# Linear attention with a gated MLP: a mixed second-stage list, maxima copies on VectorE, k and q by half batch

## The chip, the cores and the metric

The kernel runs on one core of a Trainium2 chip. The metric is the device time of one execution in microseconds (us); lower is better. A profiled execution gives the trace from which all rows below come. Engines are named as the profile names them: PE is TensorE's matmuls, PEld its weight loads, DVE is VectorE, ACT is ScalarE, POOL is GpSimd, SP is SyncE, which here only issues DMAs.

## What is computed

Eight batches of eight heads, 576 tokens, head size 64. First an attention with exponential features, then a gated MLP over the 512 joined columns.

```
phi(x)  = [exp(p), exp(-p)],  p = x @ w_phi - max|x @ w_phi|     # 64 -> 128 -> 256 features
kv      = phi(k)^T @ v ;  z = sum over tokens of phi(k)
x       = (phi(q) @ kv) / (phi(q) @ z + 1e-6)                    # per head
h       = relu(x @ w_in) ;  u, v = the two halves of h           # 512 -> 1024
v_n     = (v - mean) / sqrt(var + 1e-6)
out     = (u * (w_spatial @ v_n + b_spatial)) @ w_out
```

## The kernel before

Of a batch's 576 tokens, 512 are the main part, four blocks of 128, and 64 are the tail; the tails of two batches make one tile of 128. The first stage works in 36 **units**: per batch four head pairs (`pj` 0 to 3), and per pair of batches one tail unit. A loop over steps runs, at step i, the keys and queries of unit i, the maxima of unit i-1, the features and sums of unit i-2, the attention of unit i-3 and the output transpose of unit i-4 (`ORDER`, `LAGS`, lines 588 to 593). A middle step lasts some 6.7 us.

**Loads.** k and q of a batch come in bfloat16 through casting DMAs on POOL's queue, one DMA of all eight heads each (`load`, L90), into tiles with two buffers each; v comes in float32 through SP (`load_v`). They are issued 6 and 5 steps before the batch's first unit, those of a tail 5 and 4 steps before its unit (lines 650 to 676). Batches 0 and 1, the tails, are transposed on PE (`a_transpose`, L227). From batch 2 on, SP issues a DMA transpose of the whole batch's k and one of q, three steps ahead (`cross`, L105), into kT_b and qT_b, and one step before each unit a copy of half of qT into another tile (`q_even`, L223).

**Maxima.** For the units of batches 2 to 7 (`merged`), the eight heads' maxima of q, in a high and a low part, go through a PE transpose and are copied into spare partitions of two tiles that are the moving operands of the feature matmuls (L325): VectorE copies the odd one out of PSUM (L311), then POOL copies the odd one into the even one (L312).

**The second stage** of a batch is a list of tasks, made when its first stage ends (`b_tasks`, L571) and appended to one queue. After each kind of first-stage work, `fill` (L597) adds a credit in proportion to the queue's length and takes tasks from the front while the credit is at least half of the next one's cost (some 0.85 us for four matmuls of 512 columns). A task of cost 0 goes with whatever is ahead of it. The tasks are: v projections (four blocks and the tail: matmuls L428, ReLU L430, statistics L431 and L432), the normalise (a root on POOL, L438 to L441, and four multiply-adds on POOL, L445), u projections (four, L482, ReLU L484, into uT, which has one buffer), the u tail, spatial products (four, each of five matmuls, L503 and L504, which read all four normalised blocks; gate on VectorE, L506), the spatial tail, and output projections (four, L528; an odd batch adds the tail's). The copies of outputs out of PSUM alternate between VectorE and ACT (L531). Output projections of a batch are held back into the next batch's list.

**Order.** [...]DMA issues marked with `pin` keep the order of the program; other instructions are ordered ahead of time by a scheduler, mostly as the program has them. All matmul outputs share eight PSUM banks.

Of the kernel before, what the change touches and what calls it, by code (L numbers as in the profile page):

```python
# [8 lines left out]
FP32 = mybir.dt.float32  # L9
BF16 = mybir.dt.bfloat16  # L10
# [6 lines left out]
def kernel(  # L17
# [42 lines left out]
    def pin(start):  # L60
        return lambda *a, **kw: tc.keep_in_program_order(start(*a, **kw))

    def main_ap(t, b, h0=0, n=H):
        return bass.AP(tensor=t.tensor, offset=t.offset + (b * H + h0) * S * D,
                       ap=[[NB * D, P], [S * D, n], [1, NB * D]])
# [9 lines left out]

    def alloc(b):
        st[b] = dict(
            q=ld.tile([P, H, NB * D], BF16, tag="q_bf", name="q_bf", bufs=2),
            k=ld.tile([P, H, NB * D], BF16, tag="k_bf", name="k_bf", bufs=2),
            v=ld.tile([P, H * NB, D], FP32, tag="v_f", name="v_f"),  # L80
        )

# [4 lines left out]
            v=ld.tile([P, H, D], FP32, tag="v_tl", name="v_tl", bufs=1),  # L87
        )

    def load(x, b, h0=0, n=H):  # L90
        if b not in st:
            alloc(b)
        pin(nc.gpsimd.dma_start)(out=st[b][x][:, h0:h0 + n], in_=main_ap(q if x == "q" else k, b, h0, n))

    def load_v(b, eng):
        pin(eng.dma_start)(out=st[b]["v"].rearrange("p (h c) d -> p h (c d)", h=H), in_=main_ap(v, b))

    def load_tail(x, g):
        if g not in gs:
# [2 lines left out]
        for i in range(2):  # L102
            pin(eng.dma_start)(out=gs[g][x][i * TL:(i + 1) * TL], in_=tail_ap(t, 2 * g + i))

    def cross(b):  # L105
        d = st[b]
        for x in ("k", "q"):
            d[x + "T"] = ld.tile([P, 2 * H, P], BF16, tag=x + "T_b", name=x + "T_b", bufs=2)
            pin(nc.sync.dma_start_transpose)(out=d[x + "T"], in_=d[x].rearrange("p h x -> p (h x)"))


    wphi_f = cpool.tile([P, F], FP32)
# [32 lines left out]
    pin(nc.vector.tensor_scalar)(out=sel, in0=sel1.unsqueeze(2).to_broadcast([P, H, F]), scalar1=-1.0,  # L145
                                 scalar2=None, op0=ALU.mult)
    for x in ("k", "q"):
        pin(nc.vector.tensor_copy)(out=st[0][x][:, 0:2], in_=first[x])
    vst, vnt = [], []
    for i in range(2):  # L150
        t = cpool.tile([P, 2, 2, H, DA], BF16, name=f"vst{i}")
# [7 lines left out]
        for bl, row in ((0, TL), (1, 0)):  # L159
            pin(nc.scalar.copy)(out=t[:, bl, :], in_=ident[:, row:row + 1].to_broadcast([P, HALF]))  # L160
        vnt.append(t)
    load_v(0, nc.sync)
    for x in ("k", "q", "v"):
        load_tail(x, 0)
    load("k", 0, 2, 2)
    load("q", 0, 2, 2)
    load("k", 0, 4, 4)
    load("q", 0, 4, 4)

    w_in_bf = cpool.tile([P, KC, DFF], BF16)  # L170
    w_out_bf = cpool.tile([P, KC, DM], BF16)
    wsp = s2.tile([P, NB, T0], BF16, tag="vn", name="wsp", bufs=2)
    wspr = cpool.tile([P, NB, TL], BF16)
    wspt = ld.tile([TL, S], BF16, tag="kT_b", name="wspt", bufs=2)
    bsp_row = ld.tile([P, S], FP32, tag="qT_b", name="bsp_row", bufs=2)
    nc.sync.dma_start(out=bsp_row[TL:TL + 1, :], in_=moe_b_spatial)
    nc.sync.dma_start(out=bsp_row[0:1, :], in_=moe_b_spatial)

# [43 lines left out]

    def q_even(u):  # L223
        u["qE"] = qts[u["i"] % len(qts)]
        pin(nc.sync.dma_start)(out=u["qE"][0:D], in_=st[u["b"]]["qT"][0:D, 4 * u["pj"]:4 * u["pj"] + 4, :])

    def a_transpose(u):  # L227
        src = st[u["b"]] if u["pair"] else gs[u["g"]]
        if "kT" in src:
            for x in ("kT", "qT"):  # L230
                u[x] = src[x][:, 4 * u["pj"]:4 * u["pj"] + 4, :] if u["pair"] else src[x]
            return
        for x, copy in (("k", nc.vector.tensor_copy if u["i"] < EK else nc.scalar.copy), ("q", nc.vector.tensor_copy)):
            pt = psum.tile([P, 4, P], BF16, tag="bank", name="pt")
            for j in range(4):
                if u["pair"]:
                    blk = src[x][:, 2 * u["pj"] + j // 2, (j % 2) * P:(j % 2 + 1) * P]
                else:
                    blk = src[x][:, 2 * j:2 * j + 2, :]
                nc.tensor.transpose(out=pt[:, j, :], in_=blk, identity=ident)  # L240
            u[x + "T"] = a1.tile([P, 4, P], BF16, tag="kT", name="kT") if x == "k" else qts[u["i"] % len(qts)]
            copy(out=u[x + "T"], in_=pt)
# [63 lines left out]
    def a_max_t(u):  # L306
        pt = psum.tile([P, P], BF16, tag="bank", name="pt")
        nc.tensor.transpose(out=pt, in_=mhl[u["i"] % NM], identity=ident)
        if merged(u):
            odd, even = u["qT"][0:2 * H], u["qE"][D:D + 2 * H]  # L310
            nc.vector.tensor_copy(out=odd, in_=pt[0:2 * H, :].unsqueeze(1).to_broadcast([2 * H, 4, P]))  # L311
            nc.gpsimd.tensor_copy(out=even, in_=odd)  # L312
            return
        nc.vector.tensor_copy(out=mT[u["i"] % NM][0:2 * H, :], in_=pt[0:2 * H, :])

# [118 lines left out]
    def root(mv, r, n):  # L434

        var = small.tile([P, NB, 1], FP32, tag="var", name="var")
        rs = small.tile([P, NB, 2], FP32, tag="rs", name="rs")
        nc.gpsimd.tensor_scalar(out=var[r, 0:n], in0=mv[r, 0:n, 1:2], scalar1=1e-6, scalar2=None, op0=ALU.add)  # L438
        nc.gpsimd.tensor_tensor(out=rs[r, 0:n, 0:1], in0=var[r, 0:n], in1=neghalf[r, 0:n].unsqueeze(2), op=ALU.pow)
        nc.gpsimd.tensor_tensor(out=var[r, 0:n], in0=mv[r, 0:n, 0:1], in1=rs[r, 0:n, 0:1], op=ALU.mult)  # L440
        nc.gpsimd.tensor_scalar(out=rs[r, 0:n, 1:2], in0=var[r, 0:n], scalar1=-1.0, scalar2=None, op0=ALU.mult)  # L441
        return rs

    def normalize(dst, src, rs):
        nc.gpsimd.tensor_scalar(out=dst, in0=src, scalar1=rs[:, 0:1], scalar2=rs[:, 1:2],  # L445
                                op0=ALU.mult, op1=ALU.add)

    def b_v(b, j):
        d = st[b]
        if j == 0:  # L450
            d["vn"] = s2.tile([P, NB, HALF], BF16, tag="vn", name="vn", bufs=2)
            d["mv"] = small.tile([P, NB, 2], FP32, tag="mv", name="mv")
            d["vr"] = {}
        d["vr"][j] = s2.tile([P, HALF], BF16, tag="vr", name="vr", bufs=5)
        stats = small.tile([P, 6], FP32, tag="stats", name="stats")
        v_mm(lambda kc: d["xT"][:, kc, j * P:(j + 1) * P], d["vr"][j], slice(0, P), stats, d["mv"][:, j, :])

    def b_ln(b):
        d = st[b]
        rstd = root(d["mv"], slice(0, P), NB)  # L460
        for j in range(NB):
            normalize(d["vn"][:, j, :], d["vr"][j], rstd[:, j, :])

    def b_v_tail(g, bls):
        d = gs[g]
        r = slice(bls[0] * TL, (bls[-1] + 1) * TL)
        vr = s2.tile([P, HALF], BF16, tag="vr", name="vr", bufs=5)
        stats = small.tile([P, 6], FP32, tag="stats", name="stats")
        mv = small.tile([P, 1, 2], FP32, tag="mv_t", name="mv_t")
        v_mm(lambda kc: d["xTt"][:, kc, r], vr, r, stats, mv[:, 0, :])  # L470
        rstd = root(mv, r, 1)
        for bl in bls:
            r = slice(bl * TL, (bl + 1) * TL)
            normalize(vnt[g % 2][r, bl, :], vr[r], rstd[r, 0, :])
# [90 lines left out]
    def out_tasks(b):  # L565
        ts = [(MM, lambda j=j: b_o(b, j)) for j in range(NB)]
        if b % 2:
            ts.append((MM, lambda: b_o_tail(b // 2, [0, 1])))
        return ts

    def b_tasks(b):  # L571

        g, bl = b // 2, b % 2
        held = out_tasks(b - 1) if b else []
        ts = held[:2]
        ts.append((MM, lambda: b_v_tail(g, [bl])))
        ts += [(MM, lambda j=j: b_v(b, j)) for j in range(NB)]
        ts.append((0.0, lambda: b_ln(b)))
        ts += held[2:]
        if b == 0:  # L580
            ts += [(0.3, lambda i=i: transpose_spatial(i)) for i in range(NB + 1)]
        ts += [(MM, lambda dc=dc: b_u(b, dc)) for dc in range(KC)]
        ts.append((MM / 2, lambda: b_u_tail(g, [bl])))
        ts += [(MS, lambda dc=dc: b_s(b, dc)) for dc in range(KC)]
        ts.append((MS / 2, lambda: b_s_tail(g, [bl])))
        return ts + (out_tasks(b) if b == B - 1 else [])

# [65 lines left out]
    def at(i, f, *a):  # L653
        io.setdefault(i, []).append(lambda: f(*a))

    at(1, load, "k", 1)
    at(1, load, "q", 1)
    at(1, load_v, 1, nc.sync)
    at(2, load_weight, w_in_bf[:, :, HALF:DFF], cols[:, :, HALF:DFF])
    at(3, load_weight, wsp, rows[:, :, 0:T0])  # L660
    at(3, load_weight, wspr, rows[:, :, T0:S])
# [2 lines left out]
    at(4, load_weight, w_in_bf[:, :, 0:HALF], cols[:, :, 0:HALF])  # L664
    at(4, load_weight, w_out_bf, moe_w_out.rearrange("(kc p) f -> p kc f", p=P))
    for u in units:
        if not u["pair"] and u["g"] > 0:
            at(u["i"] - AT, load_tail, "k", u["g"])
            at(u["i"] - AT + 1, load_tail, "q", u["g"])
            at(u["i"] - AT + 1, load_tail, "v", u["g"])  # L670
        if u["pair"] and u["pj"] == 0 and u["b"] > 1:
            at(u["i"] - AB, load, "k", u["b"])
            at(u["i"] - AB + 1, load, "q", u["b"])
            at(u["i"] - AB + 1, load_v, u["b"], nc.sync)
            if u["b"] >= XB:
                at(u["i"] - XP, cross, u["b"])
    at(7, weights_with_max)
    for u in units:
        if merged(u):
# [37 lines left out]
```

## Time and profile before

| | us |
|---|---|
| median of 13 runs | 288.94 |
| lowest to highest | 286.95 to 298.14 |
| the profiled execution's own time | 288.7 |
| its span, first to last instruction | 286.9 |
| POOL: vs multiplies (L287), 64 of 1.04 us | 65.4 |
| POOL: even maxima copies (L312), 24 of 0.60 us | 14.5 |
| POOL: issuing k and q of the main part (L61), 18 | 16.3 |
| POOL: normalises (L445), 32 of 0.77 us | 24.2 |
| DMA: median from issue to landing, k_bf / q_bf / kT_b / qT_b / xT | 8.0 / 7.5 / 6.6 / 4.8 / 3.4 |

A row of a profile's groups has the line, the engine and the operation, the tile written and those read, the shapes and the number of instructions. A row of waits has who waited for whom, the microseconds in total, how often, and the longest. A row of the timeline has start and duration in us. A row of a stretch has, after its bounds and its length, the busy time of PE, PEld, DVE, ACT and POOL with instruction counts, the granted clock, the DMA share and GB/s.

### The profile page before, as it was taken

What the parts mean: (1) busy time and instruction counts of PE and PEld (TensorE: products, weight loads), DVE (VectorE), ACT (ScalarE), POOL (GpSimd) and SP (SyncE); (2) the same over time, 40 slices, a digit from 0 to 9 for tenths busy, and PEclk for the clock granted to TensorE, in tenths of its full rate; (3) what the DMA queues carried; (4) which work ended last, traced back from release to release, by engine and by line L of the source; (5) the groups of instructions that cost most, each with busy time, mean ns of one, the idle gap of its engine ahead of it and who ended that gap; (6) DMA issues with size and microseconds to landing.
All of it is one profiled execution on the core that took longest, in us unless ns stands there. A gap on an engine that the chain in (4) does not pass through costs nothing.

```text
span 286.9 us, 8120 instructions
## 1 busy us (share of the span) xinstructions
PE 259.0 (90%) x3042; PEld 171.7 (60%) x3042; DVE 220.6 (77%) x551; ACT 222.4 (77%) x504; POOL 203.1 (71%) x368
## 2 busy tenths in 40 slices
PE   3168899989899989999999989999999999999993
PEld 2057776766576565667666666666666775554441
DVE  6279998878698967899798968887879796655441
ACT  7649999998598996899889977899879967833601
POOL 8569998089966998789858996789568953420710
PEclk9999999999999999999999999999999999999999
DMA  7989999999555998999939998999732211212105
GB/s 182 215 161 121 208 220 222 167 196 163 71 99 156 218 210 91 152 302 165 194 84 146 257 187 148 223 160 178 161 110 66 68 20 73 75 39 74 74 2 184
DMA packets 83628, 41.90 MB, mean 146 GB/s; under 512 B 50626, under 2 KB 78978, under 8 KB 83588
## 3 DMA queue, kind: packets, MB, share of 16 engines
q1 hardware_dynamic: 56100, 29.90, 46.9%
q0 software_dynamic: 27328, 11.41, 33.3%
q8 instruction: 24, 0.39, 0.6%
q14 instruction: 16, 0.13, 0.2%
q10 hardware_dynamic: 160, 0.07, 0.1%
HBM read 32.85 MB, written 9.44 MB: 147 GB/s over the span
## 4 chain that ended last, share of the span: by engine, by line
PE 56%; POOL 14%; DVE 12%; ACT 9%; DMA 4%; issue 3%; POOLq 0%; ACTq 0%; DVEq 0%
PE ps L503 8%; PE po L528 8%; PE pv L428 7%; PE pu L482 6%; PE ps L247 5%; DMA q_tl<-in_q_dram 4%; PE pv L359 4%; ACT kf L262 4%; ACT qf L346 3%; PE pq L325 3%; PE pn L379 3%; POOL vn L445 3%; DVE mk L259 3%; DVE stats L431 2%; PE ps L504 2%
## 5 line engine op out<-in xcount | busy, mean ns | idle before, releaser
L262 ACT ACTIVATE kf<-ps 128x512 bf16<-128x512 f32 x144 | 75.5, 644 | 9.3 <-DVE mk L259 9.1
L287 POOL TENSOR_TENSOR vs<-v_f,em 128x512 bf16<-128x512 f32 x64 | 65.4, 1042 | 17.0 <-ACT em L282 11.6
L346 ACT ACTIVATE qf<-pq 128x512 bf16<-128x512 f32 x128 | 66.3, 617 | 11.2 <-PE pq L325 10.7
L259 DVE TENSOR_REDUCE mk<-ps 128x4 f32<-128x512 f32 x72 | 45.8, 672 | 0.6 <-PE ps L247 0.3
L273 DVE TENSOR_REDUCE mq<-ps 128x4 f32<-128x512 f32 x62 | 39.6, 678 | 4.9 <-PE ps L247 4.1
L503 PE MATMUL ps<-w_spT,vn 128*128 128x512 bf16 x128 | 34.3, 380 | 2.9 <-POOL vn L445 2.9
L506 DVE TENSOR_TENSOR uT<-ps,uT 128x512 bf16<-128x512 f32 x32 | 22.0, 687 | 19.2 <-PE ps L504 19.2
L431 DVE BATCH_NORM_STATS2 stats<-vr 128x6 f32<-128x512 bf16 (+1 forms) x40 | 26.7, 681 | 7.0 <-ACT vr L430 6.7
L482 PE MATMUL pu<-xT,w_in_bf 128*128 128x512 bf16 x128 | 31.4, 379 | 0.3 <-ACT kf L262 0.3
L528 PE MATMUL po<-w_out_bf,uT 128*128 128x512 bf16 x128 | 31.4, 379 | 0.0
L428 PE MATMUL pv<-w_in_bf,xT 128*128 128x512 bf16 x128 | 31.2, 379 | 0.0
L430 ACT ACTIVATE vr<-pv 128x512 bf16<-128x512 f32 (+1 forms) x40 | 23.7, 629 | 7.3 <-PE pv L428 6.6
L370 DVE TENSOR_TENSOR x<-pn,rc 128x256 bf16<-128x256 f32 x64 | 25.1, 419 | 0.5
L359 PE MATMUL pv<-vs,kf 128*128 128x66 bf16 x512 | 24.5, 193 | 0.6 <-DVE mq L273 0.4
L445 POOL TENSOR_SCALAR vn<-vr,rs 128x512 bf16<-128x512 bf16 x32 | 24.2, 766 | 0.8
L379 PEld LDWEIGHTS <-qf 128*128 128x128 bf16 x512 | 20.0, 97 | 7.9 <-ACT qf L346 1.1
L531 ACT COPY ob<-po 128x512 f32<-128x512 f32 x18 | 11.2, 621 | 16.3 <-PE po L528 10.0
L484 ACT ACTIVATE uT<-pu 128x512 bf16<-128x512 f32 x32 | 19.5, 638 | 5.3 <-PE pu L482 5.1
L359 PEld LDWEIGHTS <-kf 128*128 128x128 bf16 x512 | 21.8, 97 | 2.9 <-issue 2.0
L379 PE MATMUL pn<-kv,qf 128*128 128x66 bf16 x512 | 21.7, 193 | 0.9 <-ACT qf L346 0.9
L361 PE MATMUL pv<-vst,kf 128*128 128x66 bf16 x128 | 21.2, 192 | 1.1 <-POOL vst L304 1.1
L302 POOL TENSOR_TENSOR vst<-v_tl,em 64x512 bf16<-64x512 f32 x16 | 16.3, 1037 | 5.5 <-ACT em L282 5.3
(128 smaller groups left out, 563.0 us busy)
## 6 DMA issues: line engine op xcount, KB each, us to landing
v_f<-in_v_dram SPq DMA_DIRECT2D x8, 1024.0 KB, 10.5
out_dram<-ob SPq DMA_DIRECT2D x32, 256.0 KB, 2.6
k_bf<-in_k_dram POOLq DMA_DIRECT2D x7, 512.0 KB, 8.0
q_bf<-in_q_dram POOLq DMA_DIRECT2D x7, 512.0 KB, 7.5
qt<-qT_b SPq DMA_DIRECT2D x24, 64.0 KB, 3.7
v_tl<-in_v_dram SPq DMA_DIRECT2D x8, 128.0 KB, 7.5
w_in_bf<-in_moe_w_in_dram POOLq DMA_DIRECT2D x2, 512.0 KB, 8.3
out_dram<-ob SPq DMA_DIRECT2D x8, 128.0 KB, 2.4
```

The costliest lines, as they stand in the source:

```text
L259: nc.vector.tensor_reduce(out=u["mk"][:, hs], in_=pk, axis=AX.X, op=ALU.max, apply_absolute_value=True)
L262: nc.scalar.activation(out=u["kf"][:, s, hs, :], in_=pk, func=AF.Exp, bias=0.0, scale=sc)
L273: nc.vector.tensor_reduce(out=mq[:, 4 * half:4 * half + 4], in_=pq, axis=AX.X, op=ALU.max, apply_absolute_value=True)
L287: nc.gpsimd.tensor_tensor(out=vs[:, s, :, 0:D], in0=st[u["b"]]["v"][:, pj * H:(pj + 1) * H, :], in1=em[:, s, :].unsqueeze(2).to_broadcast( ...
L346: nc.scalar.activation(out=qf[:, s], in_=pq, func=AF.Exp, bias=0.0, scale=sc)
L359: nc.tensor.matmul(out=pv[:, hh, s, :], lhsT=u["kf"][:, s, 4 * hh + c, :], rhs=u["vs"][:, s, 4 * hh + c, :], start=(c == 0), stop=False)
L379: nc.tensor.matmul(out=pn[:, pos, :], lhsT=u["qf"][hh][:, s, pos, :], rhs=d["kv"][:, 2 * u["pj"] + hh, s, :], start=(s == 0), stop=(s == 1))
L428: nc.tensor.matmul(out=pv[r], lhsT=lhs(kc), rhs=w_in_bf[:, kc, HALF:DFF], start=(kc == 0), stop=(kc == KC - 1))
L445: nc.gpsimd.tensor_scalar(out=dst, in0=src, scalar1=rs[:, 0:1], scalar2=rs[:, 1:2], op0=ALU.mult, op1=ALU.add)
L482: nc.tensor.matmul(out=pu, lhsT=w_in_bf[:, kc, dc * P:(dc + 1) * P], rhs=d["xT"][:, kc, :], start=(kc == 0), stop=(kc == KC - 1))
L503: nc.tensor.matmul(out=ps, lhsT=d["vn"][:, sp, cs], rhs=w_spT[:, sp, 0:T0], start=(sp == 0), stop=False)
L528: nc.tensor.matmul(out=po[r], lhsT=lhs(dc), rhs=w_out_bf[:, dc, :], start=(dc == 0), stop=(dc == KC - 1))
```

## The change

Four things. (1) The list of a batch is ordered anew: the held outputs stand one by one ahead of the v tail, between the second and third v projection, and in turns with normalises and u projections; the root and the four normalises are tasks of their own. (2) The even copy of the maxima is made by VectorE. (3) k and q of batches 1 to 7 are loaded as two DMAs of four heads, into four half-size tiles per tensor with a buffer each, used in turns, one DMA a step; v of batches 2 to 7 comes as two DMAs, into the same tile. The tail loads of batches 4 and 6 (with 5 and 7) start one step earlier. (4) The DMA transposes are made per unit, three steps before it, 48 of a quarter of the size. Two small weight tiles that shared buffers with kT_b and qT_b share them with other tiles.

```diff
-        st[b] = dict(q=ld.tile([P, H, NB * D], BF16, tag="q_bf", bufs=2), k=..., v=...)
+        st[b] = dict(q=[None, None], k=[None, None], v=...)
...
+    def half_tile(x, b, y):
...
+            n = f"{x}_bf{(2 * b + y) % 4}"
+            st[b][x][y] = ld.tile([P, 4, NB * D], BF16, tag=n, name=n, bufs=1)
...
-    def cross(b):
-        d = st[b]
-        for x in ("k", "q"):
-            d[x + "T"] = ld.tile([P, 2 * H, P], BF16, tag=x + "T_b", name=x + "T_b", bufs=2)
-            pin(nc.sync.dma_start_transpose)(out=d[x + "T"], in_=d[x].rearrange("p h x -> p (h x)"))
+    def cross(x, u):
+        n = f"{x}T_b{u['b'] % 2}{u['pj']}"
+        u[x + "T"] = ld.tile([P, 4, P], BF16, tag=n, name=n, bufs=1)
+        src = st[u["b"]][x][u["pj"] // 2][:, 2 * (u["pj"] % 2):2 * (u["pj"] % 2) + 2, :]
+        pin(nc.sync.dma_start_transpose)(out=u[x + "T"], in_=src.rearrange("p h x -> p (h x)"))
...
-            nc.gpsimd.tensor_copy(out=even, in_=odd)
+            nc.vector.tensor_copy(out=even, in_=odd)
...
-        held = out_tasks(b - 1) if b else []
-        ts = held[:2]
-        ts.append((MM, lambda: b_v_tail(g, [bl])))
-        ts += [(MM, lambda j=j: b_v(b, j)) for j in range(NB)]
-        ts.append((0.0, lambda: b_ln(b)))
-        ts += held[2:]
+        outs = out_tasks(b - 1) if b else []
+        vs = [(MM, lambda j=j: b_v(b, j)) for j in range(NB)]
+        us = [(MM, lambda dc=dc: b_u(b, dc)) for dc in range(KC)]
+        ss = [(MS, lambda dc=dc: b_s(b, dc)) for dc in range(KC)]
+        ns = [(0.0, lambda j=j: b_ln(b, j)) for j in range(NB)]
+        ts = outs[:1] + [(MM, lambda: b_v_tail(g, [bl]))] + vs[:2] + outs[1:2] + vs[2:]
+        ts.append((0.0, lambda: b_root(b)))
         if b == 0:
             ts += [(0.3, lambda i=i: transpose_spatial(i)) for i in range(NB + 1)]
-        ts += [(MM, lambda dc=dc: b_u(b, dc)) for dc in range(KC)]
-        ts.append((MM / 2, lambda: b_u_tail(g, [bl])))
-        ts += [(MS, lambda dc=dc: b_s(b, dc)) for dc in range(KC)]
+        for y in range(NB):
+            ts += ns[y:y + 1] + outs[2 + y:3 + y] + us[y:y + 1]
+        ts += [(MM / 2, lambda: b_u_tail(g, [bl]))] + ss
...
-    at(1, load, "k", 1)
-    at(1, load, "q", 1)
+    at(1, load, "k", 1, 0)
+    at(1, load, "q", 1, 0)
+    at(1, load, "k", 1, 1)
+    at(1, load, "q", 1, 1)
...
+            early = 1 if u["g"] > 1 else 0
+            at(i - AT - early, load_tail, "k", u["g"])
+            for x in ("q", "v"):
+                at(i - AT + 1 - early, load_tail, x, u["g"])
+        if u["pair"] and u["b"] >= XB:
+            if u["pj"] == 0:
+                for n, (x, y) in enumerate((("k", 0), ("q", 0), ("k", 1), ("q", 1))):
+                    at(i - AB + n, load, x, u["b"], y)
+                for y in range(2):
+                    at(i - AB + 1 + 2 * y, load_v, u["b"], y)
+            for x in ("k", "q"):
+                at(i - XP, cross, x, u)
```

More of the change, by code (lines that the diff above doesn't have):

```diff
@@ L77, in alloc @@
         st[b] = dict(
-            q=ld.tile([P, H, NB * D], BF16, tag="q_bf", name="q_bf", bufs=2),
-            k=ld.tile([P, H, NB * D], BF16, tag="k_bf", name="k_bf", bufs=2),
+            q=[None, None], k=[None, None],
             v=ld.tile([P, H * NB, D], FP32, tag="v_f", name="v_f"),
@@ L88, in alloc_tail, with load, load_v @@
         )
-    def load(x, b, h0=0, n=H):
+    def half_tile(x, b, y):
         if b not in st:
             alloc(b)
-        pin(nc.gpsimd.dma_start)(out=st[b][x][:, h0:h0 + n], in_=main_ap(q if x == "q" else k, b, h0, n))
-    def load_v(b, eng):
-        pin(eng.dma_start)(out=st[b]["v"].rearrange("p (h c) d -> p h (c d)", h=H), in_=main_ap(v, b))
+        if st[b][x][y] is None:
+            n = f"{x}_bf{(2 * b + y) % 4}"
+            st[b][x][y] = ld.tile([P, 4, NB * D], BF16, tag=n, name=n, bufs=1)
+        return st[b][x][y]
+    def load(x, b, y, h0=0, n=4):
+        t = half_tile(x, b, y)
+        pin(nc.gpsimd.dma_start)(out=t[:, h0:h0 + n], in_=main_ap(q if x == "q" else k, b, 4 * y + h0, n))
+    def load_v(b, y=None):
+        if b not in st:
+            alloc(b)
+        h0, n = (0, H) if y is None else (4 * y, 4)
+        pin(nc.sync.dma_start)(
+            out=st[b]["v"][:, h0 * NB:(h0 + n) * NB, :].rearrange("p (h c) d -> p h (c d)", h=n),
+            in_=main_ap(v, b, h0, n))
     def load_tail(x, g):
@@ L147 @@
     for x in ("k", "q"):
-        pin(nc.vector.tensor_copy)(out=st[0][x][:, 0:2], in_=first[x])
+        pin(nc.vector.tensor_copy)(out=half_tile(x, 0, 0)[:, 0:2], in_=first[x])
     vst, vnt = [], []
@@ L161 @@
         vnt.append(t)
-    load_v(0, nc.sync)
+    load_v(0)
     for x in ("k", "q", "v"):
         load_tail(x, 0)
[L165 to L168, printed above, removed]
+    load("k", 0, 0, 2, 2)
+    load("q", 0, 0, 2, 2)
+    load("k", 0, 1)
+    load("q", 0, 1)
     w_in_bf = cpool.tile([P, KC, DFF], BF16)
@@ L173 @@
     wspr = cpool.tile([P, NB, TL], BF16)
-    wspt = ld.tile([TL, S], BF16, tag="kT_b", name="wspt", bufs=2)
-    bsp_row = ld.tile([P, S], FP32, tag="qT_b", name="bsp_row", bufs=2)
+    wspt = s2.tile([TL, S], BF16, tag="ob", name="wspt", bufs=6)
+    bsp_row = s2.tile([P, S], FP32, tag="xT", name="bsp_row", bufs=3)
     nc.sync.dma_start(out=bsp_row[TL:TL + 1, :], in_=moe_b_spatial)
@@ L224, in q_even @@
         u["qE"] = qts[u["i"] % len(qts)]
-        pin(nc.sync.dma_start)(out=u["qE"][0:D], in_=st[u["b"]]["qT"][0:D, 4 * u["pj"]:4 * u["pj"] + 4, :])
+        pin(nc.sync.dma_start)(out=u["qE"][0:D], in_=u["qT"][0:D])
     def a_transpose(u):
+        if u["pair"] and u["b"] >= XB:
+            return
         src = st[u["b"]] if u["pair"] else gs[u["g"]]
[L229 to L232, printed above, removed]
         for x, copy in (("k", nc.vector.tensor_copy if u["i"] < EK else nc.scalar.copy), ("q", nc.vector.tensor_copy)):
@@ L236, in a_transpose @@
                 if u["pair"]:
-                    blk = src[x][:, 2 * u["pj"] + j // 2, (j % 2) * P:(j % 2 + 1) * P]
+                    blk = src[x][u["pj"] // 2][:, 2 * (u["pj"] % 2) + j // 2, (j % 2) * P:(j % 2 + 1) * P]
                 else:
@@ L456, in b_v, with b_root, b_ln @@
         v_mm(lambda kc: d["xT"][:, kc, j * P:(j + 1) * P], d["vr"][j], slice(0, P), stats, d["mv"][:, j, :])
-    def b_ln(b):
+    def b_root(b):
+        st[b]["rs"] = root(st[b]["mv"], slice(0, P), NB)
+    def b_ln(b, j):
         d = st[b]
-        rstd = root(d["mv"], slice(0, P), NB)
-        for j in range(NB):
-            normalize(d["vn"][:, j, :], d["vr"][j], rstd[:, j, :])
+        normalize(d["vn"][:, j, :], d["vr"][j], d["rs"][:, j, :])
     def b_v_tail(g, bls):
@@ L654, in at @@
         io.setdefault(i, []).append(lambda: f(*a))
-    at(1, load, "k", 1)
-    at(1, load, "q", 1)
-    at(1, load_v, 1, nc.sync)
+    at(1, load, "k", 1, 0)
+    at(1, load, "q", 1, 0)
+    at(1, load, "k", 1, 1)
+    at(1, load, "q", 1, 1)
+    at(1, load_v, 1)
     at(2, load_weight, w_in_bf[:, :, HALF:DFF], cols[:, :, HALF:DFF])
@@ L666 @@
     for u in units:
+        i = u["i"]
         if not u["pair"] and u["g"] > 0:
[L668 to L676, printed above, removed]
+            early = 1 if u["g"] > 1 else 0
+            at(i - AT - early, load_tail, "k", u["g"])
+            for x in ("q", "v"):
+                at(i - AT + 1 - early, load_tail, x, u["g"])
+        if u["pair"] and u["b"] >= XB:
+            if u["pj"] == 0:
[5 more added lines that the diff above has]
+                at(i - XP, cross, x, u)
     at(7, weights_with_max)
```

## The prediction

> **What bounds the kernel now.** I read the shares of busy time first, then the busy time by stretch, then the list of waits, then the timeline around the longest of them.
>
> ```profile
> PE 259.0 (90%) x3042; PEld 171.7 (60%) x3042; DVE 220.6 (77%) x551; ACT 222.4 (77%) x504; POOL 203.1 (71%) x368
> ```
>
> TensorE (PE) is busiest, but its ends are modelled, so the stretches say more. The columns are length, then PE, PEld, DVE, ACT and POOL busy.
>
> ```profile
> 0.00:20.00 20.00, 7.78 (x46) 5.13 (x47) 10.44 (x33) 12.15 (x21) 13.14 (x30) 1.00 1.08 199
> 20.00:60.00 40.00, 35.96 (x533) 28.60 (x532) 37.38 (x106) 37.29 (x89) 31.15 (x49) 1.00 1.20 177
> 60.00:80.00 20.00, 17.25 (x201) 11.67 (x199) 14.52 (x38) 15.08 (x35) 18.75 (x35) 1.00 0.82 139
> 80.00:110.00 30.00, 27.91 (x360) 18.94 (x358) 24.98 (x61) 25.61 (x62) 24.29 (x44) 1.00 0.94 173
> 110.00:160.00 50.00, 49.71 (x606) 33.51 (x606) 43.42 (x104) 44.41 (x103) 40.94 (x76) 1.00 0.96 168
> 170.00:260.00 90.00, 89.44 (x1065) 58.12 (x1063) 71.98 (x177) 71.16 (x161) 58.75 (x109) 1.00 0.55 109
> ```
>
> From 110 us on PE is the bound: 49.7 of 50 and 89.4 of 90. It idles 12.2 us in the first 20 (the first loads), 4.0 in the opening up to 60, 2.8 in 60:80, where POOL is busy 18.75 of 20, and 2.1 in 80:110. A change that moves no matmul can win only there and in the short waits of later batches. The waits name the cause:
>
> ```profile
> POOL k_bf L61 <- DMA kT_b<-k_bf: 6.6, 1, 6.6
> PEld L503 <- POOL vn L445: 5.7, 9, 0.8
> PE ps L503 <- POOL vn L445: 2.9, 8, 0.5
> PE pq L325 <- POOL qt L312: 2.1, 2, 1.4
> ```
>
> Where TensorE waits in the middle, it waits for POOL. Two pieces of the timeline:
>
> ```profile
> 71.55 0.39 PE L503 MATMUL ps<-w_spT,vn 128*128 128x512 bf16 x1 [0.53 <-POOL vn L445]
> 72.31 0.39 PE L503 MATMUL ps<-w_spT,vn 128*128 128x512 bf16 x1 [0.36 <-POOL vn L445]
> 73.06 0.39 PE L503 MATMUL ps<-w_spT,vn 128*128 128x512 bf16 x1 [0.36 <-POOL vn L445]
> 73.81 0.39 PE L503 MATMUL ps<-w_spT,vn 128*128 128x512 bf16 x1 [0.36 <-POOL vn L445]
> ```
>
> Four matmuls start 0.76 us apart, where running ones of this size start 0.22 apart: 4 x 0.54 = 2.2 us lost for batch 0's normalised values. POOL was late because it stood 6.64 us before the k load of batch 3, issued at 57.85.
>
> ```profile
> 101.48 0.27 PE L325 MATMUL pq<-qt,wm 128*128 128x128 bf16 x2 [1.43 <-POOL qt L312]
> ```
>
> Here TensorE waits for the even copy of the maxima, which had stood on POOL behind a root.
>
> [...]at 71.55 to 73.81 the row looks half busy, yet it delivers a third of its rate. [...]a quarter-size one (xT) lands in 3.4 us, the full one (kT_b) in 6.6[...].
>
> **The change, part by part.** Sum against the profiled execution's own 288.7 us (span 286.9 and 1.8 around it), which is 0.24 below the median of 288.94.
>
> *Even copies to VectorE.* They take 24 x 0.602 = 14.5 us off POOL. The two waits of TensorE for qt, 2.1 us, go: the new copy follows the odd one on the same engine. **Gain 2.1** (bounds 1.5 to 2.1). [...]Queued behind it are the key and query maxima that ACT's Exps and the next transposes wait for. [...]At 87% (110:160) TensorE lost next to nothing; at 93% (20:60) it lost 10%, mostly for other causes. I take **1.2 us on the path**, bounds 0 and 6.
>
> *Half loads.* Batches 1 to 7: 28 issues for 14. A full issue takes POOL 0.93 (median of k_bf), the half ones at the start took 0.80: 28 x 0.80 - 14 x 0.93 = +9.4 us on POOL, so net 9.4 - 14.5 = -5.1. In the opening the four issues of batch 1 add 1.3 us to a POOL that is almost never idle from 20 to 48; TensorE there waits for ACT and VectorE more, so **cost 0.4** (0 to 1.3). The first half of batch 1's q lands earlier: TensorE waited 0.8 us for it at 31: **gain 0.6** (0 to 0.8). The k load of batch 3 no longer shares a two-buffer tag with batch 2 but has its own buffer, last read by TensorE's transposes of batch 1, done by 45.2. Then POOL's 6.64 us should go and with it the 2.2 us for batch 0's vn: **gain 2.0** (0 to 2.2). The tail loads of batches 4 and 6 move a step ahead of the k load: before, six issues, 4.8 us of POOL, stood between 150 and 161, its root came 5.4 us after its statistics, and TensorE lost 2 x 0.54 at 168 to 169: **gain 1.0** (0 to 1.1).
>
> *Transposes.* 48 of a quarter size for 12 full ones; SP's issue time goes from 43.9 us (the sum of the 12) to 48 x 1.25 (median of xT) = 60, plus 6 v halves at 0.55: +19 us of SP over 190. Moved past on SP: outputs, xT and q_even. Each pair's transposes start three steps, some 20 us, before its keys; landing 3.4 hides. Cost 0; without that cover, up to 2.
>
> *The list.* Matmuls are the same. Up to the last v, and from there to the spatial product, the same tasks stand: the last v to the spatial product is 5.6 us of second-stage matmuls in both lists. Only the normalises move: n3 was queued right after the last v, some 11.5 us ahead of the spatial product (155.47 to 167.16 in batch 3); now only u3 and the u tail lie between, 1.33/5.6 x 11.5 = 2.7 us. n3 takes 0.77, so it is in time while POOL runs less than 1.95 us late. From statistics to root POOL was late by 8.7, 1.8, 1.9, 5.4, 1.7, 0.7, 0.2 and 0.15 us; the two large ones are what the loads cure. **Cost 0.6** (0 to 9). A new wait: uT has one buffer, and the fourth held output of the previous batch, which still reads it, now comes after u0; u0's ReLU waits for that output's matmuls, 0.86 us, and what lies between. Behind it on ACT stand Exps; other PSUM banks cover it. **Cost 0.6** in seven batches (0 to 6). The drain at the end (262 to 284) has the same work after its last v: 0.
>
> **Sum.** Gains 2.1 + 0.6 + 2.0 + 1.0 = 5.7; costs 1.2 + 0.4 + 0.6 + 0.6 = 2.8; 288.7 - 2.9 = **285.8 us**.
>
> **Rivals.** *Late normalises, slower.* If POOL runs 3.2 us late at n3 (a vs pair of 2.08, a load of 0.8, a mhl pair), the spatial product waits 3.2 - 1.95 = 1.25 us in seven batches, 8.8 instead of 0.6: 285.8 + 8.2 = **294.0**. For it: n3 stood ready only 0.7 to 3.7 us ahead even when queued 9 us sooner. Against: POOL loses 5 us of work and bursts are spread. It decides from a lateness of 1.95; the sum turns slower beyond 1.95 + 3.5/7 = 2.45.
> [...]
> *POOL's wait for a transpose stays, a smaller gain.* If the 6.64 us are not due to the shared buffers, 2.0 stays: **287.8**. For it: batch 3's load has no need of batch 2's buffer as I read the code, so the wait isn't understood.
> *It doesn't do what it says*: by the diff u and spatial are not in turns; all four spatial tasks still follow the u tail. No sum above counts on turns.
>
> **Chances.** Forecast 0.48; small gain 0.12; no change 0.14; slower 0.26. A measurement of this kernel tells about 0.3% from no change, 0.87 us: faster means under 288.07. That gives faster 0.48 + 0.10 = 0.58, same 0.02 + 0.14 = 0.16, slower 0.26. The likeliest case alone spans 283.5 to 287.5. All gains at no cost give 288.7 - 5.7 = 283.0, and with the other 1.0 us of 60:80 282.0; upward the range takes in a third of the slower rival's spread (290 to 297): 282.0 to 292.0.
>
> **What would show it.** Right: no wait of TensorE for qt; [...]POOL's 6.6 us wait gone and its busy time near 198; 60:80 with under 1 us idle. Wrong: waits for vn over 9 us in sum or in every batch (late normalises); [...]ACT waiting before uT for po; PE waiting for kT or qT (SP).

## The result and the profile after

The changed kernel takes **284.84 us** (median of 11 runs, 283.0 to 286.13), the kernel before, beside it, 289.33 (48 runs): the ratio is **0.985** [0.983, 0.988]. A second measurement gave 284.0, ratio 0.980 [0.978, 0.983]. The forecast was 285.8, in a range of 282 to 292, with faster as the likeliest sign. Ratios here are taken over undisturbed runs, so that one can differ a little from the quotient of the medians shown. Brackets are 95% intervals.

The profiled execution has 284.84 us, too, and a span of 283.0, 3.9 less than before. First the shares of busy time of the changed kernel:

```profile
PE 258.7 (91%) x3042; PEld 172.4 (61%) x3042; DVE 229.6 (81%) x575; ACT 223.1 (79%) x504; POOL 198.5 (70%) x358
```

VectorE has 9.0 us more than before, POOL 4.6 less. By stretch (columns as before: length, then PE, PEld, DVE, ACT, POOL):

```profile
20.00:60.00 40.00, 36.28 (x528) 28.52 (x526) 37.37 (x103) 36.85 (x91) 38.67 (x61) 1.00 1.23 170
60.00:80.00 20.00, 18.88 (x234) 13.47 (x234) 16.74 (x46) 17.31 (x40) 15.52 (x28) 1.00 0.96 151
80.00:110.00 30.00, 28.90 (x360) 19.72 (x357) 27.30 (x67) 26.72 (x63) 25.57 (x46) 1.00 1.04 169
110.00:160.00 50.00, 50.00 (x607) 33.51 (x606) 46.43 (x113) 45.14 (x106) 39.66 (x72) 1.00 1.11 169
```

The idle time of PE in 60:80 falls from 2.75 to 1.12 us, in 80:110 from 2.09 to 1.10, in 110:160 from 0.29 to none, 2.9 us in all. These are the stretches at which the prediction aimed. In a second profile of the changed kernel (after_2) they are 1.34, 1.38 and 0.53, only 1.9 us less than before, though that execution took the same time between the points compared below. So such sums of idle time are good to about 1 us. The waits of the changed kernel (L513 and L454 are the spatial product and the normalise; before they were L503 and L445):

```profile
PEld L513 <- POOL vn L454: 1.2, 2, 0.7
...
PE ps L513 <- POOL vn L454: 0.4, 1, 0.4
```

The wait of POOL for a k load (6.6 us), the waits of TensorE for qt (2.1), and most of those for vn (5.7 and 2.9 on the two PE rows) are gone. POOL's multiplies now wait 21.3 us for ACT (11.6 before): POOL has become early instead of late.

**A second measure.** The first 20 us depend on when the first loads land, and by 18 us the profiles lie up to 2.6 us apart. So I also compare points inside the traces: the end of the first ReLU of a v projection (ACT writing vr), and, as a milestone of each batch, the end of its fourth gate multiply (VectorE writing uT from ps). The changed kernel and a_copy were profiled twice; between points these repeated to 0.1 us. The kernel before was profiled once.

| kernel | first v at | batch 0 at | batch 7 at | first v to batch 0 | batch 0 to 7 |
|---|---|---|---|---|---|
| before | 51.4 | 82.2 | 278.2 | 30.8 | 196.0 |
| fixed k and q buffers (b_tags) | 51.1 | 79.7 | 275.8 | 28.6 | 196.1 |
| all but list and copy (b_half) | 51.5 | 80.1 | 275.0 | 28.6 | 194.9 |
| all but the list (a_list) | 52.9 | 82.0 | 277.3 | 29.0 | 195.3 |
| all but the copy (a_copy, a_copy_2) | 51.6, 50.9 | 80.2, 79.5 | 272.6, 271.9 | 28.6, 28.6 | 192.4, 192.4 |
| the whole change (after, after_2) | 52.1, 51.6 | 81.1, 80.7 | 274.4, 274.0 | 29.0, 29.0 | 193.3, 193.3 |

From the first v to batch 7 the change takes off 4.5 us (226.8 to 222.3). Loads and transposes give 3.3 of them (before against b_half), the list 2.5 (b_half against a_copy), and the copy costs 1.3 (a_copy against after). With the copy made first and the list after it, the copy costs 0.8 and the list gives 2.0.

### The profile page after: what moved, and what is told of

The parts are those of the page before. It is cut to its first block, busy times and chain, and to the rows that moved or that the text cites. A ratio compares the mean times of both kernels' runs of the same rounds, so it can differ in the third digit from the quotient of the medians.

```text
span 283.0 us, 8167 instructions
## 1 busy us (share of the span) xinstructions
PE 258.7 (91%) x3042; PEld 172.4 (61%) x3042; DVE 229.6 (81%) x575; ACT 223.1 (79%) x504; POOL 198.5 (70%) x358
## 3 DMA queue, kind: packets, MB, share of 16 engines
q1 hardware_dynamic: 57348, 29.90, 51.6%
## 4 chain that ended last, share of the span: by engine, by line
PE 62%; DVE 11%; DMA 9%; ACT 8%; POOL 5%; issue 2%; POOLq 0%; ACTq 0%; DVEq 0%
PE ps L513 10%; PE pv L437 9%; PE po L538 8%; PE pu L492 7%; PE ps L256 6%; DMA q_tl<-in_q_dram 4%; PE pv L368 4%; PE pn L388 4%; ACT kf L271 3%; DMA k_bf<-in_k_dram 3%; DVE mk L268 3%; PE pq L334 3%; PE ps L514 2%; DVE stats L440 2%; DMA xT<-x 2%
## 5 line engine op out<-in xcount | busy, mean ns | idle before, releaser
L296 POOL TENSOR_TENSOR vs<-v_f,em 128x512 bf16<-128x512 f32 x64 | 65.5, 1044 | 22.7 <-ACT em L291 21.3
L268 DVE TENSOR_REDUCE mk<-ps 128x4 f32<-128x512 f32 x72 | 47.7, 677 | 2.6 <-PE ps L256 1.8
L513 PE MATMUL ps<-w_spT,vn 128*128 128x512 bf16 x128 | 33.2, 379 | 0.5 <-POOL vn L454 0.4
L538 PE MATMUL po<-w_out_bf,uT 128*128 128x512 bf16 x128 | 32.4, 379 | 0.0
L492 PE MATMUL pu<-xT,w_in_bf 128*128 128x512 bf16 x128 | 32.1, 379 | 0.0
L454 POOL TENSOR_SCALAR vn<-vr,rs 128x512 bf16<-128x512 bf16 x32 | 24.3, 766 | 1.1
```

Of the source, the lines that this page charges most:

```text
L268: nc.vector.tensor_reduce(out=u["mk"][:, hs], in_=pk, axis=AX.X, op=ALU.max, apply_absolute_value=True)
L296: nc.gpsimd.tensor_tensor(out=vs[:, s, :, 0:D], in0=st[u["b"]]["v"][:, pj * H:(pj + 1) * H, :], in1=em[:, s, :].unsqueeze(2).to_broadcast( ...
L492: nc.tensor.matmul(out=pu, lhsT=w_in_bf[:, kc, dc * P:(dc + 1) * P], rhs=d["xT"][:, kc, :], start=(kc == 0), stop=(kc == KC - 1))
L513: nc.tensor.matmul(out=ps, lhsT=d["vn"][:, sp, cs], rhs=w_spT[:, sp, 0:T0], start=(sp == 0), stop=False)
L538: nc.tensor.matmul(out=po[r], lhsT=lhs(dc), rhs=w_out_bf[:, dc, :], start=(dc == 0), stop=(dc == KC - 1))
```

## Experiments

My theory: POOL's wait for a buffer and its bursts of work made normalised values and maxima late; the loads cure that, the copy on VectorE adds to it, the list costs a little. Rivals: the list by itself makes the normalises late; the copy is what pays or what hurts; POOL's wait had nothing to do with the shared buffers.

### One part of the change at a time, on the kernel before

**b_copy**: the even copy on VectorE, alone.

```diff
-            nc.gpsimd.tensor_copy(out=even, in_=odd)
+            nc.vector.tensor_copy(out=even, in_=odd)
```

> The kernel before with the even copy of the maxima on VectorE, nothing else. Own theory (POOL was late, the copy's place cost TensorE two waits): -0.9 us, the 2.1 us of waits for qt gone, some of it taken back by VectorE; POOL's 6.6 us wait stays. [...]Rival (the new list brought the gain): no change.

Measured: median 294.1, ratio 1.010 [1.007, 1.013], **slower**. No branch of the expectation had the reason. The waits for qt did go, and VectorE's copies averaged 0.37 us. But TensorE now waits for xT, the input of the v projections. From the waits of b_copy:

```profile
PE pv L428 <- DMA xT<-x: 5.8, 2, 4.1
```

Rows of POOL and of SP's queue in b_copy (start, duration):

```profile
114.01 0.95 POOL L61 DMA_DIRECT2D k_bf<-in_k_dram  x1 [0.28 <-issue]
...
114.05 2.40 SPq L61 DMA_TRANSPOSE qT_b<-q_bf  x1
...
117.79 2.78 SPq L388 DMA_TRANSPOSE xT<-x  x2
```

The same place in the kernel before:

```profile
116.65 2.72 SPq L388 DMA_TRANSPOSE xT<-x  x2
...
116.82 0.61 POOL L312 COPY qt<-qT_b 16x512 bf16<-16x512 bf16 x1
117.38 0.95 POOL L61 DMA_DIRECT2D k_bf<-in_k_dram  x1
```

In both kernels the whole-batch transpose of q stands at the head of SP's queue and waits for the load of q, and two small transposes of xT queue behind it: SP issues nothing from 105.1 to 113.59 before, and from 106.5 to 114.05 here. So this hold is not what the copy's move changed. What changed is the load of the next k. In the kernel before it stands on POOL behind a pair of vs multiplies and an even copy, and goes out 0.7 us after the first transpose of xT. Without the copy it stands ahead of the pair, and goes out 3.8 us before that transpose. From issue to landing of the first xT there, b_copy, then before:

```profile
DMA to landing us min/median/max: 7.5/7.5/7.5
...
DMA to landing us min/median/max: 3.4/3.4/3.4
```

The transpose of q takes longer to land, too, 9.2 us instead of 4.4. TensorE comes to its v projection only 0.9 us earlier than before (120.40 against 121.28); xT lands 5.2 us later (125.26 against 120.02). Two batches on it is the same: 6.7 us with the k load first, 2.5 in the kernel before with xT first. That the k load slows the transposes is read from this order; no run moved the load alone. PE in b_copy at the first place:

```profile
125.31 0.61 PE L428 MATMUL pv<-w_in_bf,xT 128*128 128x512 bf16 x1 [4.09 <-DMA xT<-x]
...
127.52 3.49 PE L428 MATMUL pv<-w_in_bf,xT 128*128 128x512 bf16 x8
```

TensorE loses 4.09 us, and then eight matmuls take 3.49, 0.44 each instead of 0.22. In 123.90:130.70 the granted clock is 0.50: half clock for 6.8 us, from 1.4 us before the wait ends. In a_ns below, a wait of 2.12 us has half clock behind it for 3.4 us (105.90 to 109.30; mean clock 0.99 over that execution), while waits of 1.76 and 2.39 us in b_tagcopy have none (mean clock 1.0 over that execution). What brings the clock down is not shown. This execution took 295.75, so its stalls are larger than the median's; the same wait stands in b_tagcopy, in an execution at its median.

**b_list**: the new list and its split of root and normalises, alone (the part on `b_tasks` of the diff above; `b_ln` is split into `b_root` and one normalise a call).

```diff
...
-        ts.append((0.0, lambda: b_ln(b)))
-        ts += held[2:]
+        ts.append((0.0, lambda: b_root(b)))
...
+        for y in range(NB):
+            ts += ns[y:y + 1] + outs[2 + y:3 + y] + us[y:y + 1]
...
```

> The kernel before with the new list of tasks, nothing else. Own theory: the list gains nothing by itself and costs up to 1.2 us, because normalises stand later behind a POOL that is still late: 0 to +1.2 us, waits for vn at least as long as before (8.6 us of both kinds). Rival (mixing the kinds brought the gain): -2 to -4 us.

Measured: 292.81, ratio 1.011 [1.006, 1.016], **slower**, by some 3 us, where at most 1.2 was expected. This is my slower rival's mechanism. The waits of b_list:

```profile
PEld L504 <- POOL vn L445: 9.8, 11, 1.7
...
PE ps L504 <- POOL vn L445: 7.2, 8, 1.4
```

And POOL in b_list between the first and the last normalise of batch 1:

```profile
103.80 0.77 POOL L445 TENSOR_SCALAR vn<-vr,rs 128x512 bf16<-128x512 bf16 x1
...
106.90 2.08 POOL L287 TENSOR_TENSOR vs<-v_f,em 128x512 bf16<-128x512 f32 x2
...
109.11 0.78 POOL L445 TENSOR_SCALAR vn<-vr,rs 128x512 bf16<-128x512 bf16 x1
...
111.72 0.77 POOL L445 TENSOR_SCALAR vn<-vr,rs 128x512 bf16<-128x512 bf16 x1
```

In the kernel before, the four ran in one piece from 101.53 to 104.55, and this same burst (two tail loads, a q load, a vs pair) came after them. With the split list it comes between them: the last starts 7.9 us after the first.

**b_tags**: two fixed buffers each for k and q, by the batch's parity, in place of two from a shared pool; whole loads and everything else as before.

```diff
-            q=ld.tile([P, H, NB * D], BF16, tag="q_bf", name="q_bf", bufs=2),
+            q=ld.tile([P, H, NB * D], BF16, tag=f"q_bf{b % 2}", name="q_bf", bufs=1),
```

(k likewise.)

> The kernel before with k and q in two fixed buffers (one for even, one for odd batches) instead of a pool of two; same loads, same memory. Own theory (the 6.6 us wait of POOL came from which buffer the pool gave out): the wait is gone and with it the late normalises of batch 0, -2.0 us. Rival (the wait belongs to the size or the time of the loads): the wait stays, no change.

Measured: 286.1, ratio 0.989 [0.984, 0.993], **faster**. POOL's wait for k_bf is gone. The stretch 60:80 in b_tags:

```profile
60.00:80.00 20.00, 18.67 (x246) 13.63 (x248) 16.78 (x41) 16.81 (x40) 14.68 (x26) 1.00 0.95 166
```

PE's idle time there is 1.33 us instead of 2.75. From the first v to batch 0 it takes 28.6 us instead of 30.8, and from there on as long as before, 196.1. The gain of 2.2 us lies where POOL's wait stood. This shows that the shared buffers caused the 6.6 us wait, and the rival "POOL's wait stays" falls. Why the pool gave batch 3's load the buffer that batch 2's transpose was still reading stays open.

### The change without one part

**b_half**: the changed kernel with the old list and the copy back on POOL, that is the loads, transposes and tail loads alone.

```diff
-            nc.vector.tensor_copy(out=even, in_=odd)
+            nc.gpsimd.tensor_copy(out=even, in_=odd)
...
-        ts.append((0.0, lambda: b_root(b)))
...
+        ts.append((0.0, lambda: b_ln(b)))
+        ts += held[2:]
...
```

> The kernel before with the loads by half batch, their times and the transposes per unit; the old list, and the even copy on POOL. Own theory: -3.2 us (0.6 in the opening, 2.0 from POOL's wait, 1.0 from batch 3's burst, 0.4 back for issues), the waits for qt stay. Rival (the list or the copy brought the gain): within 1 us of before. Rival (POOL has 9.4 us more to issue): slower by 1 us or more.

Measured: 285.61, ratio 0.986 [0.981, 0.991]. After the opening it gains 1.2 us over b_tags (194.9 against 196.1). One wait of TensorE for qt is left, 1.32 us at 99.22, behind a root on POOL.

**a_copy**: the changed kernel, but the even copy on POOL (the one-line diff of b_copy reversed).

> The changed kernel with the even copy back on POOL. Against the kernel before. If the copy is worth its 2.1 us of waits once the loads are spread: 287 us, 2 us over the changed kernel, waits of TensorE for qt of 1 to 2 us and more for vn. If the fixed buffers brought nearly all (fixed buffers alone: 0.989, loads by half alone: 0.986 of before): 0.985 to 0.988 of before. If late normalises bite once POOL has the copies too: over 0.99.

Measured: 283.17, ratio 0.977 [0.972, 0.983], under every branch of the expectation. TensorE waits for no qt, though the copy is on POOL. The normalises of batch 1 on POOL in a_copy:

```profile
98.14 0.77 POOL L454 TENSOR_SCALAR vn<-vr,rs 128x512 bf16<-128x512 bf16 x1
98.85 0.88 POOL L61 DMA_DIRECT2D q_bf<-in_q_dram  x1
99.78 2.26 POOL L454 TENSOR_SCALAR vn<-vr,rs 128x512 bf16<-128x512 bf16 x3
```

Between the first normalise and the last now stands one half load of 0.88 us, where b_list had a burst of 4.5 us (104.57 to 109.11). b_half and a_copy differ by the list alone: 194.9 against 192.4. **With loads by half, the list gains 2.5 us.**

**a_list**: the changed kernel with the old list (`b_tasks` and `b_ln` as before, the copy on VectorE).

```diff
...
-        ts.append((0.0, lambda: b_root(b)))
...
+        ts.append((0.0, lambda: b_ln(b)))
+        ts += held[2:]
...
```

> The changed kernel with the old list (half loads and the copy on VectorE stay). If the list costs something behind a POOL that is no longer late: 0.6 to 1.2 us faster than the changed kernel, 0.981 to 0.984 of before. If mixing the kinds pays once POOL is on time: slower than the changed kernel, 0.987 or more. The copy shows no wait of TensorE for xT here if transposes per unit are what keeps SP free.

Measured: 286.06, ratio 0.987 [0.982, 0.992], between milestones 195.3. The list is worth 2.0 us by this pair. One wait for xT is left, against the expectation:

```profile
PE pv L437 <- DMA xT<-x: 0.8, 1, 0.8
```

Here, too, a half load of k goes out before that xT (113.74 and 114.23), and xT lands after 7.3 us.

**a_burst**: the halves issued two in one step, as k and q were, and the tail loads not earlier.

```diff
-                    at(i - AB + n, load, x, u["b"], y)
+                    at(i - AB + n % 2, load, x, u["b"], y)
...
-            early = 1 if u["g"] > 1 else 0
+            early = 0
```

> The changed kernel with the half loads issued two at a time in the old steps (k at 6, q at 5 steps before) and the tail loads at their old steps: same DMAs, not spread. Own step (spreading cures batch 3's burst): +1.0 us over the changed kernel, waits for vn in batch 3. Rival (only the buffers matter): equal to the changed kernel within 0.5 us.

Measured: 286.35, ratio 0.988 [0.983, 0.993], between milestones 194.9: after batch 0, spreading the loads and the tails is worth 1.6 us. Before it one wait of 1.9 us for maxima from POOL stands at 44 us, behind a pair of k loads. The waits for vn that I expected in batch 3 stand in batch 1 (107 to 108 us) instead. Two waits of PE for xT, 1.4 us in all, are there too. Of the waits of a_burst:

```profile
PEld L513 <- POOL vn L454: 2.9, 5, 0.8
```

**b_tagcopy**: b_tags and the copy on VectorE (the two diffs above together).

> The kernel before with fixed buffers for k and q and the even copy on VectorE; whole-batch loads and transposes. If the copy's own gain of 2.1 us shows once POOL is not late: 284 us, 0.982 of before. If the copy alone was slower because TensorE then meets transposes of x that are queued on SP behind a whole-batch q transpose waiting for its load: 0.99 to 1.0 of before, TensorE waiting for xT again by 2 us or more.

Measured: 288.62, ratio 0.994 [0.990, 0.997]: of the gain of b_tags, about half is lost. The number was expected, but not for the reason that I gave, the queue on SP. Its waits for xT are b_copy's, in an execution of 288.52:

```profile
PEld L428 <- DMA xT<-x: 5.1, 2, 2.9
```

At both places the k load goes out ahead of xT (by 1.8 and 2.7 us), and xT lands after 7.1 and 5.8 us; in b_tags it comes 0.8 and 2.4 us behind, and xT lands after 3.4 and 3.0. So the copy's move is bad with whole-batch loads and transposes even where POOL is on time. In the changed kernel no wait for xT is in the list.

### What the list and the copy need

**after_2** and **a_copy_2** repeat the changed kernel and a_copy, on one chip.

> The changed kernel again, on the same chip as the three others of this set. 0.983 to 0.988 of before, as in the result.

> The changed kernel with the even copy on POOL, again. If the copy on VectorE costs time in the changed kernel too, as its first run says (0.977 against 0.985 from another chip): 1 to 3 us under the changed kernel beside it, milestones of the batches drawing apart from batch 1 on. If that was the chip or chance: within 0.5 us of the changed kernel.

Measured: 284.0, ratio 0.980 [0.978, 0.983], a little under what was expected, and 283.41, ratio 0.978 [0.975, 0.981]. The times alone do not separate the two, for the intervals overlap. The traces do: 192.4 twice against 193.3 twice between milestones, and 221.0 twice against 222.3 twice from the first v. a_copy is the best version measured: the change without its move of the copy.

**b_taglist**: b_tags and the new list (b_list's diff with b_tags's).

> The kernel before with fixed buffers and the new list; whole-batch loads and transposes, copy on POOL. If the list was slower alone only since POOL was late from its 6 us wait: now at or under the fixed buffers alone, 0.978 to 0.988 of before. If it needs the spread half loads, because load issues stand between the normalises: over the fixed buffers alone, 0.992 or more, waits for vn of 6 us or more in sum.

Measured: 288.09, ratio 0.994 [0.992, 0.996], above b_tags (0.989), though the ends of the intervals overlap. From the waits of b_taglist (an execution of 290.69, above its median, with a wait of 3.2 us for kT_b besides):

```profile
PEld L504 <- POOL vn L445: 6.3, 7, 1.6
```

POOL's wait for a buffer is gone here, and the normalises are late still. A POOL that is on time is not enough for the list. With the halved and spread issues between its normalises it gains.

**a_ns**: the changed kernel with the four normalises right behind the root, outputs and u still in turns.

```diff
         ts.append((0.0, lambda: b_root(b)))
+        ts += ns
...
-            ts += ns[y:y + 1] + outs[2 + y:3 + y] + us[y:y + 1]
+            ts += outs[2 + y:3 + y] + us[y:y + 1]
```

> The changed kernel with the four normalises queued right behind the root, the rest of the new list kept. If late normalises still cost 0.6 us: that much under the changed kernel. If POOL is on time now (waits for vn 1.7 us in all): within 0.3 us of it. If the normalises in a bunch hold up POOL's other work again: over it by up to 1 us.

Measured: 287.07, ratio 0.991 [0.988, 0.994], 3.1 us above after_2, where up to 1 us was expected. From the trace of a_ns:

```profile
96.93 3.03 POOL L454 TENSOR_SCALAR vn<-vr,rs 128x512 bf16<-128x512 bf16 x4
99.92 0.87 POOL L61 DMA_DIRECT2D q_bf<-in_q_dram  x1
100.04 2.98 DVE L321 COPY qt<-qT_b 16x512 bf16<-16x512 bf16 x1
100.81 2.06 POOL L296 TENSOR_TENSOR vs<-v_f,em 128x512 bf16<-128x512 f32 x2
...
104.39 0.41 PE L388 MATMUL pn<-kv,qf 128*128 128x66 bf16 x8 [2.12 <-DVE mq L282]
```

Four normalises in one piece push the rest of POOL's work together. VectorE's copy, 0.285 us at the median, takes 2.98 us here, until 0.15 us after POOL's vs multiplies end, and the query maximum behind it makes TensorE wait 2.12 us, with half clock after it. From batch 0 to batch 1 this kernel takes 35.9 us, the changed one 32.5. So the split of the normalises is the part of the list that must stay if the copy is on VectorE.

## Why the prediction was right, and where its steps were not

The sign was right, and so was the main mechanism, POOL made late by a wait for a shared buffer; the sum was near (285.8 against 284.84 and 284.0). The gain, put at 2.9 us, is 4.3 to 5.7 (1.5 and 2.0% of the kernel before). **Two terms of the sum had the wrong sign**: the list was 3.2 to 3.7 us better than put down, the copy 1.7 to 2.2 worse. They cancel to 1.5 us, most of what the sum lacked. That it came so near is in part luck.

*The buffers (predicted 2.0): right.* In b_tags the stretch from the first v to batch 0 is 2.2 us shorter, just what the prediction read as lost there. The times give 1.1% ± 0.5, 3.3 us.

*The opening (predicted gain 0.6, cost 0.4): neither is to be seen.* From the transposes of k at 18 us to the first v, 33.1 us pass in the kernel before, in b_tags, in b_half and in both profiles of the changed kernel, though POOL is busy 38.67 us in 20:60, 7.5 more than before. The wait of TensorE for q at 31 (0.65 us on the PE row) is gone, in b_tags too, which loads q whole; a wait of 0.69 for kT from VectorE stands in its place.

*Spread tail loads (predicted 1.0): the size was near, the place in part another.* b_half is 1.2 us better than b_tags after the opening, but 0.9 of that lies between batches 0 and 1. In batch 3, where the gain was to come, the waits for vn (1.15 us in b_tags) are gone from b_half, but a wait of 0.82 us for a small DMA on SP stands there instead. The whole change does gain 1.0 us between the milestones of batches 2 and 3 (31.0 to 30.1 and 30.0). POOL's busy time, "near 198", is 198.5.

*Transposes (predicted 0): right for the changed kernel*, which has no wait of TensorE for a DMA transpose. But the step looked only at SP's own time. b_copy and b_tagcopy show transposes that land up to 4 us later when the next k load goes out ahead of them.

*The list (predicted cost 1.2): wrong.* Measured: a gain of 2.0 to 2.5 us on the new loads, a loss on the old ones, 1.1% alone and 0.5% between the ratios of b_taglist and b_tags. Two things failed. The step counted only how much later n3 is queued, not that splitting the normalises clears POOL: in one piece they hold it for 3.0 us, with maxima and the copy behind them (a_ns). And the cost of the wait for uT, 0.6, was nothing: ACT waits before it for po 1.4 us in all (2 times), and between 105 and 216 us no wait of PE reaches 0.3 us in either profile of the changed kernel. Not all of the gain is located. 1.8 of the 2.5 us between b_half and a_copy fall between the milestones of batches 2 and 3 (30.9 against 29.1), where b_half stalls behind a small DMA on SP. From the trace of b_half:

```profile
161.40 0.41 DVE L320 COPY qT_b<-pt 16x512 bf16<-16x512 bf16 x1 [2.39 <-DMA qt<-qT_b]
...
161.87 1.02 PE L491 MATMUL pu<-xT,w_in_bf 128*128 128x512 bf16 x4 [0.82 <-DVE qT_b L320]
```

In a_copy no gap of PE of 0.3 us or more is in that stretch. That the list spaces the tasks so that this DMA lands in time is argued, not shown.

*The copy (predicted: gain 2.1, cost 1.2): the gain was booked to the wrong part.* The cost, my estimate and read from no trace, was sized well (the 87 and 93% beside it are VectorE's busy shares, 43.42 of 50 us in 110:160 and 37.38 of 40 in 20:60): with the copy on VectorE it takes 0.8 to 1.3 us more from the first v to batch 7 than with the copy on POOL. The gain is nothing in the changed kernel: in a_copy, too, the waits for qt are gone. They came from POOL's order and lateness, which loads and list cure together. In the kernel before the move did remove them, and TensorE lost more at xT, a cost that no step had: the k load that POOL then issues earlier. The copies of the changed kernel, by duration (minimum/median/maximum in ns):

```profile
L321 DVE COPY qt<-qT_b x24: 283/285/1565, 77.7 to 240.4; 16x512 bf16<-16x512 bf16 x24
```

They sum to 9.7 us, 0.40 on average, 0.12 above the median of 0.285. Nine of the 24 took longer than 0.3 us; eight of them end 0.08 to 0.16 us after an instruction of POOL. That these wait for POOL is read from those ends alone; no run separates it from another cause. The longest one, from the timeline of the changed kernel:

```profile
166.73 2.05 POOL L296 TENSOR_TENSOR vs<-v_f,em 128x512 bf16<-128x512 f32 x2
167.37 1.56 DVE L321 COPY qt<-qT_b 16x512 bf16<-16x512 bf16 x1
```

The copy ends at 168.93, just after the pair of vs multiplies (168.78).

*The rivals.* Late normalises: real in b_list and b_taglist, where the waits for vn are long in batches 1 and 3, and cured in the changed kernel (PE row 0.4 us in all). In one piece the last normalise starts 2.3 us after the first; in b_list it came 7.9 after it, so 5.6 later, in a_copy 3.1, so 0.9 later. These lie on the two sides of my 1.95, which counted POOL's lateness at n3 and so is not quite the same quantity. "60:80 with under 1 us idle" was missed narrowly, 1.12 and 1.34. That u and spatial do not go in turns holds: the diff leaves the four spatial tasks together, and no gain here rests on turns.

## What to carry to other kernels

Ask first why an engine is late: a wait behind it (here 6.6 us for a buffer chosen from a shared pool) shows up as several waits elsewhere, and each of these is removed only once, whichever edit gets the credit. Splitting a block of tasks on POOL let other work slip in between: with loads of a whole batch a burst of 4.5 us, and the kernel lost (ratio 1.011, b_list); with halves issued one a step a load of 0.88 us, and it gained 2.5 us (b_half against a_copy). Before moving work off an engine, ask what that engine will start earlier by it and what this collides with, such as a load that now goes out ahead of transposes that TensorE needs soon (b_copy: xT landed after 7.5 us instead of 3.4).

## What was not expected of the hardware

- In a_ns a copy on VectorE, 0.285 us at the median, lasted through several instructions of POOL: it started at 100.04 and ended at 103.02, through the rest of a DMA issue (to 100.79) and both vs multiplies (to 102.87). It is not always so: the copy at 221.07 in the changed kernel ended after 0.51 us, in the middle of a pair of vs multiplies. What decides is open.

```profile
220.39 2.09 POOL L296 TENSOR_TENSOR vs<-v_f,em 128x512 bf16<-128x512 f32 x2
221.07 0.51 DVE L321 COPY qt<-qT_b 16x512 bf16<-16x512 bf16 x1
```

- Two waits of TensorE cost more than themselves: with one of 4.09 us came half clock for 6.8 us (b_copy), behind one of 2.12 half clock for 3.4 (a_ns).
- The same DMA transpose of xT landed 3.4 us after its issue in the kernel before, where a load of a whole batch of k was issued 0.7 us after it, and 7.5 us in b_copy, where that load was issued 3.8 us before it.
- A small copy (16x512 bf16) takes 0.285 us on VectorE (median, changed kernel) and 0.602 on POOL (kernel before); with it on VectorE the kernel takes 0.8 to 1.3 us longer from the first v to batch 7.
